# A transformer block, forward and backward, on one core: key weights on ScalarE's queue, transposes inside the key products, grad_out products in M's buffers, two norms on ScalarE

## The chip, the core and the metric

The kernel runs on one core of one Trainium2 chip. A core has five engines that run at the same time: TensorE (PE in the profile, with its weight loads as PEld), VectorE (DVE), ScalarE (ACT), GpSimd (POOL) and SyncE (SP). Each takes its own instructions in program order. TensorE writes to PSUM; the others read PSUM or SBUF. Transfers between HBM and SBUF are issued by SP, ACT or POOL, each on a queue of its own. The metric is the device time of one execution, in microseconds (us).

## The reference

One block without batch: S = 2048 rows, D = 640 columns, H = 32 heads of 20, F = 1728; bf16 throughout.

```python
h   = x + A(layernorm(x))
out = h + B(layernorm(h))
# A: linear attention
q, k, v = split(xn @ wqkv)               # per head
phi(t)  = where(t > 0, t + 1, exp(t)) + 1e-6
kv, z   = phi(k)^T v, sum of phi(k)      # over all rows, per head
A       = (phi(q) kv / (phi(q) z + 1e-6)) @ wo
# B: gated MLP
B       = (silu(hn @ w1) * (hn @ w3)) @ w2
```

The outputs are `out` and the gradients of x, wqkv, wo, w1, w3 and w2 for a given grad_out.

## The kernel before

The rows are cut into ST = 16 tiles of P = 128, the 640 columns into DT = 5 blocks of 128 or two halves of HD = 320. The order of all instructions is written out by hand (`manual_schedule`): what stands first in the program is first on its engine. The parts that the change touches are three.

**Phase 1, from 0 to about 55 us** (the loop over t at line 480). x is loaded tile by tile. For each tile DVE computes mean and variance (`Stats.part`: two `bn_stats`, one `bn_aggr`, the epsilon), POOL the inverse root (`pow`, line 154), and DVE normalises the tile in place (`p1_norm`, line 160); the even tiles above 8 are normalised by ACT instead (`norm_act`, line 165), which needs a bias from POOL (`Stats.bias`). The normalised tile is transposed: tiles 0 to 7 by PE and a copy on ACT (`p1_tr`), tiles 8 to 15 by a transposing DMA on SP's queue (in `p1_norm`). Then come the key product (`p1_mm`, tile name big, line 260) and `phi`: exp and relu on ACT, and two steps on DVE that are held back and done in a later turn (`held`, `phi_rest`). M = pk^T xn is accumulated over all tiles (`m_part`, macc, line 402). PE also does four query tiles (`q_tile`) in this loop, and four chunks of the product grad_out w2^T (`ghh_chunk`, tile gp, line 371), whose operands g2T and w2T come by transposing DMAs.
The PSUM buffers here are the tags big (2, each of two banks), tr (2) and m (2). The gp chunks take a big buffer, and the WARM matmuls on a tile of ones, ahead of everything, take a tr buffer. SP's queue at the start is: x tiles 0 and 1, the two halves of the key weights (`load_wq(2, 3)`, `load_wq(3, 4)`, line 182), x tiles 2, 3 and 4 to 7, w2T, g2T, w2T, further x and weights.

**The end of the attention, from about 90 to 103 us** (`run(...)` at line 801). `f2_half(t, j)` computes one half of tile t of h on PE. For tiles 0 to 3, half 0 is added to x by DVE; for half 1 PE adds x through an identity matmul and ACT copies the result (line 589). DVE takes the statistics; `f2_hn(t)` normalises (DVE, line 160), `f2_ht(t)` transposes on PE (trh, line 677), and ACT copies that (line 678).

**The backward pass through the MLP, from about 406 to 543 us** (the loop over t at line 1112). `b_ghn(t)` accumulates 27 blocks from ggb, which holds the gradients of two tiles and has two buffers, in parts of 9 matmuls. The next ggb comes in two loads on SP's queue: blocks 0 to 13 (FT = 14) at even t, blocks 14 to 26 at odd t. ACT has in each step the evacuation gs, y (line 1024, `ln_rest`), the transposing DMA of g_h (`b_gT`) and, in the first ten of them, one of wo or kvT.

## Time and profile before

| | |
|---|---|
| median of 4 runs | 826.88 us (826.28 to 836.13) |
| the profiled execution | 828.8 us |
| its span | 827.1 us |
| TensorE busy | 818.4 us, 99% |
| DVE, ACT, POOL busy | 454.2, 319.0, 133.8 us |
| TensorE's waits over 0.05 us that the profile names | 4.8 us in all |
| DMA moved | 157.59 MB, mean 191 GB/s |

The span runs from the first to the last instruction on the chip. Busy time is the union of an engine's instructions; matmul ends are modelled, and a matmul that runs at a lower clock counts as busy for longer. In a timeline each row gives start, length, engine, line, operation, how many were merged, and in brackets how long the engine had been idle and what ended that. Engine names with a q are the engine's sequencer, which issues transfers. A wait for several things is put down to the one that came last.

### The profile page before, as it was taken

The numbers are of one execution on the slowest core, as the hardware profiler recorded it, in microseconds if no ns is written. First come the engines' busy times: TensorE is split into PE (matmuls) and PEld (weight loads), VectorE is DVE, ScalarE is ACT, GpSimd is POOL, SyncE is SP. The second block draws the span as 40 slices with busy tenths as digits, with TensorE's granted clock in tenths as the row PEclk, the third lists the DMA queues.
The fourth block names the chain that finished last, engine by engine and source line by source line (L and its number), as shares of the span: only waits on it lengthen the run. The fifth ranks groups of instructions, "written<-read, shape, count | busy, mean of one in ns | idle before, by whom it ended". The sixth has DMA issues, their size and how long they took to land.

```text
span 827.1 us, 14217 instructions
## 1 busy us (share of the span) xinstructions
PE 818.4 (99%) x5551; PEld 523.7 (63%) x5551; DVE 454.2 (55%) x960; ACT 319.0 (39%) x609; POOL 133.8 (16%) x196
## 2 busy tenths in 40 slices
PE   8999999999999999999999999999999999999998
PEld 5677644555555555777777777777777777555554
DVE  7849898899898656400057777772681545200000
ACT  5865778655555666011121221222212333211111
POOL 2326333233222212100001111110220000000000
PEclk9999999999999999999999999999999999999999
DMA  9789999696584465999978888458995788885781
GB/s 250 216 289 211 259 244 278 221 213 168 143 204 133 144 202 166 204 253 235 258 163 186 184 217 199 72 103 178 264 216 100 163 191 172 215 194 139 159 174 38
DMA packets 318339, 157.59 MB, mean 191 GB/s; under 512 B 235456, under 2 KB 311456, under 8 KB 318272
## 3 DMA queue, kind: packets, MB, share of 16 engines
q1 hardware_dynamic: 286256, 120.65, 63.6%
q0 software_dynamic: 7376, 24.81, 8.8%
q10 hardware_dynamic: 24640, 11.23, 6.6%
q8 instruction: 43, 0.70, 0.4%
q14 instruction: 24, 0.20, 0.1%
HBM read 48.15 MB, written 51.46 MB: 120 GB/s over the span
## 4 chain that ended last, share of the span: by engine, by line
PE 96%; DMA 2%; SPq 1%; ACT 0%; DVE 0%; issue 0%; POOL 0%; ACTq 0%
PE mm L371 20%; PE job L1198 19%; PE ghn L1000 14%; PE gxn L1356 8%; PE o L766 7%; PE gw L955 7%; PE big L260 4%; PE gwo L1085 3%; PE gr L1057 3%; PE dkv L1302 3%; PE macc L402 3%; PE at L586 2%; PE mm L260 1%; DMA g2T<-in_grad_out_dram 1%; DMA pqT<-pql 1%; PE gp L371 1%
## 5 line engine op out<-in xcount | busy, mean ns | idle before, releaser
L1198 PE MATMUL job<-gb,hnN 128*128 128x432 bf16 (+2 forms) x656 | 117.0, 342 | 0.0
L1000 PEld LDWEIGHTS <-ggb 128*128 128x128 bf16 x864 | 84.5, 98 | 32.8
L1198 PEld LDWEIGHTS <-hnN 128*128 128x128 bf16 x656 | 63.6, 98 | 53.4
L371 PE MATMUL mm<-pqT,w 128*128 128x512 bf16 x405 | 93.7, 379 | 0.0
L371 PEld LDWEIGHTS <-w 128*128 128x128 bf16 x540 | 52.5, 98 | 63.0 <-issue 1.0
L1202 ACT CAST obs<-job 128x432 bf16<-128x432 f32 (+3 forms) x61 | 29.3, 480 | 123.1 <-PE job L1198 123.1
L766 PE MATMUL o<-w,hhT 128*128 128x320 bf16 x448 | 67.5, 299 | 0.0
L1000 PE MATMUL ghn<-w13a,ggb 128*128 128x320 bf16 x448 | 63.5, 299 | 0.0
L1000 PE MATMUL ghn<-w13b,ggb 128*128 128x320 bf16 x416 | 61.4, 299 | 0.0
L371 PE MATMUL mm<-g2T,w2T 128*128 128x512 bf16 x240 | 59.6, 379 | 0.0
L766 PEld LDWEIGHTS <-hhT 128*128 128x128 bf16 x448 | 43.8, 98 | 23.6
L955 PE MATMUL gw<-g,hb 128*128 128x320 bf16 x416 | 56.8, 299 | 0.0
L1065 POOL TENSOR_TENSOR sz<-Zb,g_h 128x640 f32<-128x640 bf16 x16 | 20.2, 1261 | 199.3 <-DVE g_h L1063 199.3
L955 PEld LDWEIGHTS <-hb 128*128 128x128 bf16 x416 | 40.6, 98 | 16.0 <-issue 0.3
L1356 PE MATMUL gxn<-wqT,gT 128*128 128x320 bf16 x320 | 48.7, 299 | 0.0
L391 ACT CAST ghh<-mm 128x512 bf16<-128x512 f32 x48 | 28.1, 585 | 46.2 <-PE mm L371 40.6
L705 ACT ACTIVATE sig<-mm 128x512 bf16<-128x512 f32 x56 | 33.5, 599 | 27.9 <-PE mm L371 25.6
L371 PEld LDWEIGHTS <-w2T 128*128 128x128 bf16 x260 | 25.4, 98 | 26.1 <-issue 3.2
L1012 ACT ACTIVATE gs<-ghn 128x640 bf16<-128x640 f32 x16 | 11.2, 703 | 79.0 <-PE ghn L1000 79.0
L260 PE MATMUL big<-wqkv,pqT 128*128 128x320 bf16 x260 | 39.7, 301 | 1.0 <-ACT pqT L256 0.6
L260 PEld LDWEIGHTS <-pqT 128*128 128x128 bf16 x320 | 30.7, 98 | 14.3 <-ACT pqT L256 2.1
L1356 PEld LDWEIGHTS <-gT 128*128 128x128 bf16 x320 | 31.3, 98 | 12.2
(201 smaller groups left out, 1284.6 us busy)
## 6 DMA issues: line engine op xcount, KB each, us to landing
hh_d<-hhT SPq DMA_DIRECT2D x24, 256.0 KB, 2.6
gg_d<-gate POOLq DMA_DIRECT2D x24, 256.0 KB, 4.0
gg_d<-ghh POOLq DMA_DIRECT2D x24, 256.0 KB, 3.4
ggb<-gg_d SPq DMA_DIRECT2D x6, 896.0 KB, 5.4
ggb<-gg_d SPq DMA_DIRECT2D x6, 832.0 KB, 7.3
x_sb<-in_A_x_dram SPq DMA_DIRECT2D x7, 640.0 KB, 6.9
out_dram<-obs ACTq DMA_DIRECT2D x39, 108.0 KB, 3.1
ggb<-gg_d SPq DMA_DIRECT2D x2, 1728.0 KB, 13.2
```

Of the source, the lines that this page charges most:

```text
L260: T.matmul(acc, lhsT=pqT[:, c, t * P:(t + 1) * P], rhs=wqkv[:, c, n0:n0 + HD], start=(c == 0), stop=(c == DT - 1))
L371: T.matmul(acc[:], lhsT=w[:, c, fc * P:(fc + 1) * P], rhs=rhs[:, c, :], start=(c == 0), stop=(c == DT - 1))
L391: A.copy(out=ghh[n // 2][:, n % 2, :], in_=acc[:])
L402: T.matmul(macc[m][j][:, 0:n], lhsT=pk_all[:, t, m * P:(m + 1) * P], rhs=x_ext[:, t, j * HD:j * HD + n], start=(t == 0), stop=(t == ST - 1))
L705: A.activation(sig[:, i, :], gp[:], AF.Sigmoid)
L766: T.matmul(o2["ps"][:, 0:HD], lhsT=hhT[c][:, fc, i * P:(i + 1) * P], rhs=w2[:, fc, j * HD:(j + 1) * HD], start=(fc == 0), stop=(fc == FT - 1))
L955: T.matmul(acc[:, j, 0:HD], lhsT=hb[b][:, t, i * P:(i + 1) * P], rhs=g2[:, t, j * HD:(j + 1) * HD], start=(t == 0), stop=(t == ST - 1))
L1000: T.matmul(acc[:, j, 0:HD], lhsT=ggb[t // 2][:, k, lo:lo + P], rhs=rhs[:, j * HD:(j + 1) * HD], start=(k == 0), stop=(k == NG - 1))
L1057: T.matmul(gr[t][:, j, 0:HD], lhsT=ghT[t][:, c, :], rhs=wT2[:, c, j * HD:(j + 1) * HD], start=(c == 0), stop=(c == DT - 1))
L1198: T.matmul(acc[:, 0:n], lhsT=lhs[:, t, m * P:(m + 1) * P], rhs=rhs(t), start=(t == 0), stop=(t == ST - 1))
L1202: A.copy(out=ob, in_=acc[:, 0:n])
L1356: T.matmul(acc[:, j, 0:HD], lhsT=g, rhs=wqT[:, k, j * HD:(j + 1) * HD], start=(k == 0), stop=(k == 14))
```

## The change

- The key weights are loaded in two halves from ACT's queue (`load_wk`), ahead of ACT's table load, and no longer from SP's. On SP's queue x tiles 8 to 11 come before the second w2T load.
- WARM falls from 44 matmuls to 34, followed by 8 more after the transposes of tile 0; they take an m buffer.
- Tile 0 is only centred before its transposes (256 columns by DVE, 384 by ACT with a bias `nmean`); exp and relu apply the scale for it (`RAW = 1`), and DVE scales the tile in place at t = 3 (`p1_scale`).
- The transposes of tile t + 1 stand between the two halves of key product t, for all of tiles 1 to 7.
- The order of DVE's steps in the loop (statistics S, norm N, phi's steps R, the scale C, norms on ACT A) is a table, `v_steps`. The four gp chunks come at t = 3 to 6 and not at 2 to 5, and take an m buffer; the first query tile comes at t = 6; M's products begin at t = 7 with three tiles, then three, then one per turn. The first w1 and w3 loads come one turn later.
- `Stats.bias` is one POOL instruction and not two.
- Half (2, 0) of `f2_half` is done ahead of (0, 1); `f2_hn(1)` and `f2_hn(2)` are done by ACT.
- In the backward loop the load of blocks 14 to 26 of ggb is issued from ACT's queue, in the middle of odd turns, after `ln_rest` and `b_gT`.

```diff
@@ -162,12 +162,12 @@
 
         def norm_act(self, out, src, t):
 
-            A.activation(out=out, in_=src, func=AF.Identity, bias=self.nb[t][:, 1:2], scale=self.rs[:, t:t + 1])
+            A.activation(out=out, in_=src, func=AF.Identity, bias=self.nb[t][:, 0:1], scale=self.rs[:, t:t + 1])
 
         def bias(self, t):
-            nb = self.nb[t] = cp.tile([P, 2], F32, name="nb", bufs=4)
-            G.tensor_tensor(out=nb[:, 0:1], in0=self.mv[:, t, 0:1], in1=self.rs[:, t:t + 1], op=ALU.mult)
-            G.tensor_tensor(out=nb[:, 1:2], in0=zero[:], in1=nb[:, 0:1], op=ALU.subtract)
+            nb = self.nb[t] = cp.tile([P, 1], F32, name="nb", bufs=4)
+            G.tensor_scalar(out=nb[:], in0=self.mv[:, t, 0:1], scalar1=self.rs[:, t:t + 1], scalar2=-1.0, op0=ALU.mult,
+                            op1=ALU.mult)
 
     ln1, ln2 = Stats("ln1"), Stats("ln2")
 
@@ -184,10 +184,13 @@
     def load_x(a, b):
         dma(out=x_sb[:, a:b, :], in_=xS[:, a:b, :])
 
+    def load_wk(j):
+        A.dma_start(out=wqkv[:, :, D + j * HD:D + (j + 1) * HD], in_=wq_v[:, :, D + j * HD:D + (j + 1) * HD])
+
+    load_wk(0)
     load_x(1, 2)
+    load_wk(1)
     A.activation(sg[:], zero[:], AF.Exp)
-    load_wq(2, 3)
-    load_wq(3, 4)
     load_x(2, 3)
     load_x(3, 4)
     load_x(4, 8)
@@ -235,7 +238,8 @@
     Z = cp.tile([P, DT], F32, name="Z")
 
     XT_DMA = 8
-    WARM = 44
+    WARM = 34
+    RAW = 1
 
     def on_act(t):
         return t > XT_DMA and t % 2 == 0
@@ -255,15 +259,21 @@
 
             A.copy(out=pqT[:, a:b, t * P:(t + 1) * P], in_=tr[:, a:b, :])
 
+    def p1_scale(t):
+        xn = x_sb[:, t, :]
+        V.tensor_scalar(out=xn, in0=xn, scalar1=ln1.rs[:, t:t + 1], scalar2=None, op0=ALU.mult)
+
     def p1_half(acc, t, n0):
         for c in range(DT):
             T.matmul(acc, lhsT=pqT[:, c, t * P:(t + 1) * P], rhs=wqkv[:, c, n0:n0 + HD], start=(c == 0),
                      stop=(c == DT - 1))
 
-    def p1_mm(t, n0):
+    def p1_mm(t, n0, between=None):
         acc = ps.tile([P, 2, 512], F32, name="big", bufs=2)
         for j in range(2):
             p1_half(acc[:, j, 0:HD], t, n0 + j * HD)
+            if j == 0 and between is not None:
+                between()
         return acc
 
     def two(ap):
@@ -271,17 +281,16 @@
 
     held = []
 
-    def phi(acc, dst, then=None):
+    def phi(acc, dst, t):
 
         mq, rq = (p1.tile([P, D], BF16, name=n, bufs=b) for n, b in (("mq", 3), ("rq", 3)))
-        A.activation(two(mq[:]), acc[:, :, 0:HD], AF.Exp)
-        A.activation(two(rq[:]), acc[:, :, 0:HD], AF.Relu)
+        kw = dict(scale=ln1.rs[:, t:t + 1]) if t < RAW else {}
+        A.activation(two(mq[:]), acc[:, :, 0:HD], AF.Exp, **kw)
+        A.activation(two(rq[:]), acc[:, :, 0:HD], AF.Relu, **kw)
 
         def rest():
             V.tensor_scalar(out=mq[:], in0=mq[:], scalar1=1.0, scalar2=1e-6, op0=ALU.min, op1=ALU.add)
             V.tensor_tensor(out=dst, in0=mq[:], in1=rq[:], op=ALU.add)
-            if then is not None:
-                then()
         held.append(rest)
 
     def phi_rest(keep=0):
@@ -303,7 +312,7 @@
 
     def q_tile(t):
         q_home(t)
-        phi(p1_mm(t, 0), pqs[t])
+        phi(p1_mm(t, 0), pqs[t], t)
 
     dz = {}
 
@@ -432,39 +441,59 @@
     zero_pads()
     load_w2T(0, 2 * P)
     load_g2T(0)
+    load_x(8, 12)
     load_w2T(2 * P, 4 * P)
-    load_x(8, 12)
     load_wq(0, 2)
     load_x(12, ST)
-    warm = ps.tile([P, 512], F32, name="warm", tag="tr", bufs=2)
-    for _ in range(WARM):
-        T.matmul(warm[:, 0:P], lhsT=ones[:], rhs=ones[:], start=True, stop=True, skip_group_check=True)
-    ln1.run(x_sb, 0, 1)
-    ln1.part(x_sb, 1, 0)
-    for a, b in ((0, 2 * P), (2 * P, D)):
-        ln1.norm(x_sb[:, 0, a:b], x_sb[:, 0, a:b], 0)
+    def warm_up(n):
+        warm = ps.tile([P, 512], F32, name="warm", tag="m", bufs=2)
+        for _ in range(n):
+            T.matmul(warm[:, 0:P], lhsT=ones[:], rhs=ones[:], start=True, stop=True, skip_group_check=True)
+
+    warm_up(WARM)
+    def center(t, a=0, b=D):
+        ln1.center(x_sb[:, t, a:b], x_sb[:, t, a:b], t)
+
+    nmean = cp.tile([P, 1], F32, name="nmean")
+
+    def center_first():
+        V.tensor_scalar(out=nmean[:], in0=ln1.mv[:, 0, 0:1], scalar1=-1.0, scalar2=None, op0=ALU.mult)
+        center(0, 0, 2 * P)
+        A.activation(out=x_sb[:, 0, 2 * P:], in_=x_sb[:, 0, 2 * P:], func=AF.Identity, bias=nmean[:, 0:1])
+
+    def stat(t):
+        ln1.run(x_sb, t, t + 1)
+        if on_act(t):
+            ln1.bias(t)
+
+    ln1.part(x_sb, 0, 0)
+    ln1.part(x_sb, 0, 1, center_first)
     p1_tr(0, ((0, 2), (2, DT)))
-    for t in (1, 2):
-        if t == 1:
-            ln1.part(x_sb, t, 1)
-            p1_norm(t)
-            ln1.run(x_sb, t + 1, t + 2)
-        else:
-            ln1.part(x_sb, t + 1, 0)
-            p1_norm(t)
+    warm_up(8)
+    stat(1)
+    ln1.part(x_sb, 2, 0)
+    p1_norm(1)
+    ln1.part(x_sb, 2, 1)
+    ln1.part(x_sb, 3, 0)
+    p1_norm(2)
     ln1.part(x_sb, 3, 1)
+    ln1.part(x_sb, 4, 0)
+    p1_norm(3)
+    ln1.part(x_sb, 4, 1)
     w13 = [go for c0, c1 in ((0, 2), (2, 4), (4, 5)) for go in load_w13(c0, c1)]
     w13 += [lambda: dma(out=w1[:, :, F:FP], in_=rows(B_w3)[:, :, F - FL:F])]
 
     def load_wo():
         dma(out=wo[:], in_=A_wo.rearrange("(c p) n -> p c n", p=P))
 
-    trickle = {3: w13[0], 4: w13[1], 11: lambda: load_wq(4, 6), 12: w13[2], 14: w13[3], 15: load_wo}
-
-    stat_of = {t: (t + 4,) for t in range(7)}
-    stat_of.update({7: (11, 12), 8: (13,), 9: (14,), 10: (15,)})
-    norm_of = {t: (t + 3,) for t in range(8)}
-    norm_of.update({8: (11, 12), 9: (13,), 10: (14,), 11: (15,)})
+    trickle = {4: w13[0], 5: w13[1], 11: lambda: load_wq(4, 6), 12: w13[2], 14: w13[3], 15: load_wo}
+
+    R = None
+    v_steps = {1: (R, ("N", 4)), 2: (("S", 5), R, ("N", 5)), 3: (("S", 6), R, ("N", 6), ("C", 0)),
+               4: (("S", 7), R, ("N", 7), ("S", 8)), 5: (R, ("N", 8), ("S", 9)), 6: (R, ("N", 9), ("S", 10)),
+               7: (("S", 11), R, R, ("A", 10), ("N", 11)), 8: (("S", 12), R, R, ("S", 13), ("A", 12)),
+               9: (("N", 13), R, ("S", 14)), 10: (R, R, ("S", 15), ("A", 14)), 11: (("N", 15), R)}
+    V_OPS = {"S": stat, "N": p1_norm, "C": p1_scale}
 
     def xn_out(g, q):
         sl = slice(g * TPC, (g + 1) * TPC)
@@ -476,30 +505,26 @@
 
     outs = {6: ((group_out, 0),), 7: ((xn_out, 0, dma),), 10: ((group_out, 1), (xn_out, 1, dma)), 13: ((group_out, 2),)}
 
-    QT = (5, 7, 9, 11)
+    QT = (6, 7, 9, 11)
+    M0 = {7: (0, 1, 2), 8: (3, 4, 5)}
+    M0.update({t: (t - 3,) for t in range(9, ST)})
     for t in range(ST):
-        k = p1_mm(t, D)
-        if t < 3:
-            p1_tr(t + 1, ((0, 2), (2, DT)))
-        for n in stat_of.get(t, ()):
-            ln1.run(x_sb, n, n + 1)
-            if on_act(n):
-                ln1.bias(n)
-        for n in norm_of.get(t, ()):
-            if not on_act(n):
-                p1_norm(n)
-        phi_rest(t < 4)
-        phi(k, pk_all[:, t, :])
-        for n in norm_of.get(t, ()):
-            if on_act(n):
-                p1_norm(n)
+        k = p1_mm(t, D, (lambda: p1_tr(t + 1)) if t + 1 < XT_DMA else None)
+        steps = v_steps.get(t, (R,) * len(held))
+        for step in steps:
+            if step is R:
+                held.pop(0)()
+            elif step[0] != "A":
+                V_OPS[step[0]](step[1])
+        phi(k, pk_all[:, t, :], t)
+        for step in steps:
+            if step is not R and step[0] == "A":
+                p1_norm(step[1])
         if t in QT:
             q_tile(QT.index(t))
-        if 2 <= t < 6:
-            ghh_chunk(t - 2, ps.tile([P, 2, 512], F32, name="gp", tag="big", bufs=2)[:, 0])
-            p1_tr(t + 2)
-        if t >= 3:
-            m_part(0, [t - 3])
+        if 3 <= t < 7:
+            ghh_chunk(t - 3, ps.tile([P, 512], F32, name="gp", tag="m", bufs=2))
+        m_part(0, M0.get(t, ()))
         if t >= 11:
             V.memset(bd[:, t - 11, :], 0.0)
             make_mask(t - 11)
@@ -658,10 +683,14 @@
         pqs[t] = pf.tile([P, D], BF16, name="pql", bufs=4)[:]
         dma(out=pqs[t], in_=pq_v[:, t, :])
 
-    def f2_hn(t):
+    def f2_hn(t, on_act=False):
         hn[t] = (pf.tile([P, D], BF16, name="hn", tag="pql", bufs=4) if 2 <= t < TPC else
                  pf.tile([P, D], BF16, name="hn", bufs=2))
-        ln2.norm(hn[t][:], x_sb[:, t, :], t)
+        if on_act:
+            ln2.bias(t)
+            ln2.norm_act(hn[t][:], x_sb[:, t, :], t)
+        else:
+            ln2.norm(hn[t][:], x_sb[:, t, :], t)
         dma(out=hn_v[:, t, :], in_=hn[t][:])
 
     def f2_ht(t):
@@ -802,8 +831,8 @@
         (q_late, 12, lambda: (f2_wT(0), f2_wT(1))), (q_late, 13, lambda: (f2_wT(2), f2_wT(3))), (phi_rest,),
         (q_late, 14, lambda: f2_wT(4)), (load_x, 4, 8), (r_head, 5), (r_prod, 7), (r_store, 5, 6), (f2_m_out,),
         (f2_w_out,), (q_out, 8, 10), (q_out, 10, 14), (load_w2T, 8 * P, 10 * P), (mlp_ghh, 4), (q_late, 15),
-        (sig_table,), (f2_half, 0, 0), (f2_half, 1, 0), (f2_half, 0, 1), (f2_half, 1, 1), (f2_hn, 0), (mlp_ghh, 5),
-        (f2_half, 2, 0), (f2_hn, 1), (load_w2T, 10 * P, F), (f2_half, 2, 1), (f2_ht, 0), (f2_half, 3, 0), (f2_hn, 2),
+        (sig_table,), (f2_half, 0, 0), (f2_half, 1, 0), (f2_half, 2, 0), (f2_half, 0, 1), (f2_half, 1, 1), (f2_hn, 0),
+        (mlp_ghh, 5), (f2_hn, 1, True), (load_w2T, 10 * P, F), (f2_half, 2, 1), (f2_ht, 0), (f2_half, 3, 0), (f2_hn, 2, True),
         (f2_half, 3, 1), (f2_ht, 1), (mlp_ghh, 6), (f2_hn, 3), (f2_ht, 2), (r_red, 6), (r_inv, 6), (r_scale, 6), (r_T, 6),
         (f2_half, 4, 0), (f2_ht, 3), (mlp_ghh, 7), (f2_half, 4, 1), (r_red, 7), (r_inv, 7), (r_scale, 7), (r_T, 7),
         (r_store, 6, 8))
@@ -927,10 +956,10 @@
 
     ggb = {}
 
-    def load_gg(j, c0, c1):
+    def load_gg(j, c0, c1, q=dma):
         if c0 == 0:
             ggb[j] = ba.tile([P, NG, 2 * P], BF16, name="ggb", bufs=2)
-        dma(out=ggb[j][:, c0:c1, :],
+        q(out=ggb[j][:, c0:c1, :],
             in_=gg_d[c0 * P:c1 * P, j * 2 * P:(j + 1) * 2 * P].rearrange("(c p) w -> p c w", p=P))
 
     def gw2_tail():
@@ -1116,8 +1145,8 @@
             next(g, None)
 
         u = t - 2
-        if 2 <= t <= ST - 3:
-            load_gg(t // 2 + 1, *((FT, NG) if t % 2 else (0, FT)))
+        if 2 <= t <= ST - 3 and t % 2 == 0:
+            load_gg(t // 2 + 1, 0, FT)
         part()
         part()
         part()
@@ -1127,6 +1156,8 @@
             ln_rest.pop(t - 1)()
             if by_dma(t - 1):
                 b_gT(t - 1)
+            if 2 <= t <= ST - 3 and t % 2:
+                load_gg(t // 2 + 1, FT, NG, A.dma_start)
             if t <= 2 * DT:
                 n = (t - 1) % DT
                 dst, src = (woT, A_wo) if t <= DT else (kvN, kvT_d)
```

## The prediction

> **What bounds the kernel now.** I read the busy shares first, then TensorE's (PE's) waits, then the first 20 us slice by slice.
>
> ```profile
> PE 818.4 (99%) x5551; PEld 523.7 (63%) x5551; DVE 454.2 (55%) x960; ACT 319.0 (39%) x609; POOL 133.8 (16%) x196
> ```
>
> PE is busy in all but 8.7 of 827.1 us, and the change takes away only two of its 5551 matmuls. So it can win only idle time, or time in which PE runs slowly and still counts as busy. PE's waits:
>
> ```profile
> PE gp L371 <- DMA g2T<-in_grad_out_dram: 2.0, 1, 2.0
> PE warm L441 <- DVE zero L124: 1.1, 1, 1.1
> PE trh L677 <- DVE hn L160: 0.7, 1, 0.7
> PE big L260 <- ACT pqT L256: 0.6, 2, 0.3
> PE at L586 <- DMA Wp<-pkx: 0.4, 1, 0.4
> ```
>
> The first is the largest: the first grad_out product (gp, line 371) waits for its transposed operand. The windows of 1 us (PE, PEld, DVE, ACT, POOL busy; granted clock; DMA share; GB/s) show its second cost:
>
> ```profile
> 13.00:14.00 1.00, 0.27 (x5) 0.10 (x2) 0.93 (x5) 0.86 (x3) 0.17 (x1) 1.00 1.19 160
> 14.00:15.00 1.00, 0.00 (x0) 0.00 (x0) 1.00 (x3) 1.00 (x2) 0.68 (x1) 1.00 0.99 35
> 15.00:16.00 1.00, 0.76 (x2) 0.29 (x3) 0.93 (x5) 0.10 (x1) 0.35 (x1) 0.55 1.16 265
> 16.00:17.00 1.00, 1.00 (x4) 0.40 (x3) 0.89 (x3) 0.00 (x0) 0.33 (x1) 0.50 0.82 259
> ```
>
> Column 8 is the clock: it fell to half after the hole and is full again in the slice from 19. Five gp matmuls took 2.29 us there, 1.24 later; with the transposes and matmuls beside them that is 1.7 us more. VectorE (DVE) is busy in nearly every slice here, so it is what comes next. From 20 to 90 us PE has no hole above 0.11 us.
>
> **Part 1: loads at the start.** Now SyncE (SP) issues everything in order:
>
> ```profile
> 4.29 3.16 SPq L430 DMA_TRANSPOSE w2T<-in_B_w_dram  x1
> 7.51 4.24 SPq L223 DMA_TRANSPOSE g2T<-in_grad_out_dram  x1
> 11.79 1.40 SPq L430 DMA_TRANSPOSE w2T<-in_B_w_dram  x1
> ```
>
> g2T lands 7.6 us after its issue begins, at 15.11. Moving the two key-weight loads (L182, 0.99 us with their gap 1.04) to ScalarE's (ACT's) queue brings g2T's issue to 6.45 and its landing to 14.1. On ACT the two issues (0.4 to 0.5 us each) come ahead of the table load, which then ends at 3.1 instead of 2.1; ACT is first wanted at 4.5, so that costs nothing.
> Against this stands a rule of the Trainium skill (DMA: Bandwidth & Descriptors, "Issuing engines are not separate DMA queues"): loads issued from several engines run on the same 16 DMA engines and interleave, so only issue time is saved. The trace agrees where it can: from 4 to 9 us the DMA share is 1.05 or more at 318 to 358 GB/s, with one queue alone. By the row of issues I win the 1.04 us; by the rule no more than that, and the first x tile now shares its time with 400 KB of weights. Before, it landed at 3.13 with nothing beside it. Its delay lies between 0 and 1.3 us (400 KB at 318 GB/s); I take 0.25, since its 160 KB are few packets of a mix, and keep 1.3 for the range.
>
> **Part 2: the first tile.** It is now only centred (no wait for POOL's pow, 0.57 us), 256 columns on DVE and 384 on ACT, and phi applies the scale. The second half of its transposes moves from 5.85 to about 5.5, the first key product from 6.37 to about 6.2. WARM 34 + 8: 34 at 0.107 us end at 4.75, where the clock rose in the trace; no price.
>
> **Part 3: the loop.** In the new order PE does the transposes of tile t+1 inside key product t, the grad_out products come at t = 3 to 6, M's first products at t = 7, and the M buffers take the grad_out accumulators. What paces it is DVE: per tile two statistics 0.92, aggregate 0.24, epsilon 0.07, norm 0.36, and from t = 1 phi's two steps 0.83 (starts to starts). From the first statistics at 3.4 I get the norms of tiles 1, 2, 3, 4 at about 7.25, 9.2, 11.2 and 13.25, and of 5, 6, 7 at 15.6, 18.0, 20.8. In the trace they are:
>
> ```profile
> 12.32 0.44 DVE L160 TENSOR_SCALAR x_sb<-x_sb,ln_mv,ln_rs 128x640 bf16<-128x640 bf16 x1
> 13.90 0.44 DVE L160 TENSOR_SCALAR x_sb<-x_sb,ln_mv,ln_rs 128x640 bf16<-128x640 bf16 x1
> 15.49 0.44 DVE L160 TENSOR_SCALAR x_sb<-x_sb,ln_mv,ln_rs 128x640 bf16<-128x640 bf16 x1
> ```
>
> (tiles 3, 4, 5). So DVE's chain is hardly faster; the win is order. PE: tile 4's transposes at 13.75, key product 3 done at 14.75, the first gp right then with g2T there since 14.1, done at 15.85. In the trace the same work (key products 0 to 3, transposes 0 to 4, one gp) is done at 19.6 + 0.3. **Win: 4.0 us**, and the ACT hole of 0.11 at 35 us too: 4.1. Afterwards PE is the pace again (key product 1.36, transposes 0.28, gp 1.08 against DVE's 2.4 per tile).
> Does it last? Tile 8's transposed x is wanted at 28.7, issued at 23.6 and lands in 2.6 to 3.8 us; tile 9's has about 1 us left, tile 15's 3. The next far cover is mT for kvT_block(0): it landed at 67.0 and was used at 68.9. SP's chain there starts from ACT's norm of tile 14 (42.4), which comes 3.8 us earlier, so 1.6 us of cover remain. No new stall; if one, under 1 us. The two nb instructions on POOL become one (0.2 to 0.4 us, hidden).
>
> **Part 4: norms 1 and 2 of the second layernorm on ACT.** The reordered half (2,0) covers the Wp wait: -0.4. But ACT is first in, first out, and each norm now stands ahead of the copy of the next tile's half, on which the next statistics wait. On the trace's clock: epsilon of tile 1 ends at 95.65, pow 0.55, the new bias 0.2 to 0.4 on POOL, so ACT's norm starts at 96.6. Its length:
>
> ```profile
> 33.08 0.92 ACT L165 ACTIVATE x_sb<-x_sb,nb,ln_rs 128x640 bf16<-128x640 bf16 x1
> ```
>
> It holds the copy of half (2,1), ready at 96.0, until 97.4 and DVE's statistics until 97.85; so pow at 98.9, norm 2 on ACT 99.8 to 100.7, the copy of (3,1) behind it 100.6 to 101.0, statistics, pow, and hn(3) at 103.1. PE wants hn(2) at 99.2 and waits 1.5, then hn(3) and waits 1.5 again. In the trace the last transposes (trh) start at 101.33, now at 103.15: **loss 1.8 us**, the 0.4 counted in. That these norms save DVE 0.7 us wins nothing, as DVE then waits for ACT.
> Does the clock fall in these two holes? The Trainium skill (TensorE: Matmul & The Clock Gate, "What's actually happening") says that it drops after a whole idle window of about 3.4 us, and then the holes cost nothing more. The trace disagrees: one hole of 1.98 us sufficed, and cost 1.7. Two holes of 1.5 with 1.0 us of work between are near that row. Ends 0 and 1.7; I take 0.8, as it hangs on where the window falls. **Loss in all: 2.6.**
>
> **Part 5: second halves of ggb on ACT's queue.** Each of the six is 832 KB:
>
> ```profile
> ggb<-gg_d SPq DMA_DIRECT2D x6, 896.0 KB, 5.4
> ggb<-gg_d SPq DMA_DIRECT2D x6, 832.0 KB, 7.3
> ```
>
> SP issues them far ahead (424.9, landed 432.4, used at 442.2). On ACT they stand behind y and the ghT transpose of their step, and ahead of woT's:
>
> ```profile
> 434.72 1.22 ACTq L1037 DMA_TRANSPOSE ghT<-g_h  x1
> 435.98 1.30 ACTq L1133 DMA_TRANSPOSE woT<-in_A_wo_dram  x1
> 442.22 1.25 PE L1000 MATMUL ghn<-w13b,ggb 128*128 128x320 bf16 x8
> ```
>
> So issue at 435.98 and use at 442.2: 6.2 us, 9.8 us of cover becoming about 1. By the first halves' row (5.4 us, little beside them) it lands at 441.2 to 441.4, at no cost; by its own row (7.3 us, measured with the other half and the ghT transpose in flight) 1.1 us late. I take the first, since at 436 to 438.6 SP's queue is empty. The woT issue behind it delays nothing that PE waits for within a step; ghT of the odd steps lands sooner, also hidden.
>
> **Sum.** -4.1 + 1.8 + 0.8 = -1.5 us. The profiled execution took 828.8 (span 827.1 and 1.7 around it), so 827.3 there; the median of the runs, 826.88, stands 1.9 below it, and I forecast **825.4 us**.
>
> **Rivals.**
> - *ACT's norms are hidden after all* (chance 0.22): bias and copies slip between, and PE's waits of 0.7 and 0.4 go. -4.1 - 1.1: 821.7. For it: ACT is idle 0.4 to 0.9 us before most copies there. Against: strict order on ACT.
> - *The start wins little* (0.13): x shares the DMA engines with the weights and lands 1.3 us later, DVE with it, or the clock is not warm. -2.0 + 2.6: 827.5. For it: the DMA share at 1.
> - *ggb lands late* (0.15), the other side: at its own row's 7.3 us PE stalls 1.1 us in each of six pairs, a stall in one pair not helping the next: +6.6 - 1.5 = +5.1: 832.0. It decides from 6.2 us to landing on; at 7.9 us it is +8.7.
> - *The change doesn't do what it says* (0.02): the M buffers' reuse makes key products wait; about 827.
> - The forecast (0.48): 823.5 to 827.5.
>
> **Range and chances.** The range reaches from the first rival with the start's best (about 820.5) to the ggb rival's middle (830.5). A measurement of this kernel can tell about 1%, 8.3 us, from no change. Faster by that needs nearly all of PE's 8.7 idle us back: 0.04. Slower by that needs ggb at about 8 us and the rest as forecast: 0.08. Within: 0.88.
>
> **What would show it.** Right: no g2T wait on PE, full clock in the slices from 15 to 19, gp first near 14.8; ACT's two norms near 92 and 95 on the new clock with PE's trh waits at about 3 us; no wait for ggb. Wrong: PE waiting for the key weights or pqT before 10 us; PE waits on ggb (then slower); trh waits under 1 us (then near 822); a wait for mT near 64.

## The result and the profile after

The changed kernel takes **831.11 us** (median of 44 runs, 828.88 to 837.97) against 826.99 us before (63 runs): slower by 0.5%, ratio 1.0049 with a 95% interval of 1.0038 to 1.0061. The forecast was 825.4 us with a range to 830.5: it is wrong in sign, and the result lies 0.6 us outside the range.

The profiled execution took 835.1 us (span 833.4, mean granted clock 0.996) and lies above its median, so it shows more trouble than most runs have. What divides the runs is TensorE's granted clock: 28 of the 44 runs keep a mean of 0.999 or more and have a median of 830.14 us, the other 16 lie at 832.66. Of the 67 runs of the kernel before that were timed beside the first four experiments, 61 keep 0.999 or more (826.73 us). All sums below use this split. In the 18 profiles it is exact: the seven with a mean under 0.999 hold a stretch at half clock, the eleven others none between 8 us and the last 10.

First line of the busy shares after:

```profile
PE 820.3 (98%) x5549; PEld 524.0 (63%) x5549; DVE 452.8 (54%) x959; ACT 322.0 (39%) x609; POOL 133.6 (16%) x195
```

TensorE has two matmuls fewer, as counted, but is idle or slow for longer. Its waits after (line, cause: us in total, times, longest):

```profile
PE trh L706 <- DVE hn L160: 3.5, 1, 3.5
PE trh L706 <- ACT hn L165: 1.6, 1, 1.6
PE warm L451 <- DVE zero L124: 1.1, 1, 1.1
PE ghn L1029 <- DMA ggb<-gg_d: 0.9, 1, 0.9
PE tr L258 <- DVE x_sb L160: 0.6, 1, 0.6
PE big L268 <- DMA pqT<-x_sb: 0.5, 1, 0.5
PE mm L268 <- ACT mbs L418: 0.4, 1, 0.4
```

The wait for g2T is gone. In its place stand 5.1 us of trh waits in the stage with the two norms on ACT, a wait for ggb, one of the transposes of tile 1 (tr) for its norm at 7.6 us, and waits for pqT and mbs; the kernel before had no such waits but 0.7 us of trh. The start went as forecast. Windows after (PE, PEld, DVE, ACT, POOL busy; clock; DMA share; GB/s), and SP's rows (start, length of the issue):

```profile
14.00:15.00 1.00, 1.00 (x13) 0.77 (x11) 0.97 (x4) 1.00 (x3) 0.00 (x0) 1.00 1.09 345
15.00:16.00 1.00, 1.00 (x7) 0.49 (x6) 0.86 (x5) 1.00 (x3) 0.56 (x1) 1.00 1.15 98
16.00:17.00 1.00, 1.00 (x10) 0.69 (x9) 1.00 (x4) 1.00 (x2) 0.00 (x0) 1.00 2.56 182
```

```profile
3.37 3.59 SPq L439 DMA_TRANSPOSE w2T<-in_B_w_dram  x1
7.01 3.75 SPq L226 DMA_TRANSPOSE g2T<-in_grad_out_dram  x1
```

TensorE is full where it had a hole, at full clock. g2T landed at 12.83 (forecast 14.1), the first gp started at 15.08 (14.75), the norms of tiles 1 to 4 at 7.68, 9.61, 11.55 and 13.58 (7.25, 9.2, 11.2, 13.25). At the key product of tile 9, where both orders have done the same of TensorE's work but for two warm-up matmuls, the changed kernel was 3.8 us ahead of the profile of before (31.39 us against 35.23).

The end of the attention is where it was lost. First ACT before, where the copy out of PSUM (the CAST, line 589) follows PE at once (brackets: idle before, and what ended it), then ACT after, then DVE after:

```profile
96.58 0.42 ACT L589 CAST x_sb<-at 128x320 bf16<-128x320 f32 x1 [0.91 <-PE at L586]
98.35 0.42 ACT L589 CAST x_sb<-at 128x320 bf16<-128x320 f32 x1 [0.75 <-PE at L586]
```

```profile
95.01 0.92 ACT L165 ACTIVATE hn<-x_sb,nb,ln_rs 128x640 bf16<-128x640 bf16 x1 [1.02 <-POOL nb L169]
95.84 0.40 ACT L614 CAST x_sb<-at 128x320 bf16<-128x320 f32 x1
98.23 0.92 ACT L165 ACTIVATE hn<-x_sb,nb,ln_rs 128x640 bf16<-128x640 bf16 x1 [1.39 <-POOL nb L169]
99.06 0.40 ACT L614 CAST x_sb<-at 128x320 bf16<-128x320 f32 x1
```

```profile
96.28 0.49 DVE L147 BATCH_NORM_STATS2 st<-x_sb 128x6 f32<-128x320 bf16 x1 [2.07 <-ACT x_sb L614]
99.49 0.49 DVE L147 BATCH_NORM_STATS2 st<-x_sb 128x6 f32<-128x320 bf16 x1 [1.37 <-ACT x_sb L614]
103.30 0.45 DVE L160 TENSOR_SCALAR hn<-x_sb,ln_mv,ln_rs 128x640 bf16<-128x640 bf16 x1 [2.88 <-DMA pqT<-pql]
```

Each norm waits at the head of ACT's queue for POOL's bias nb, and the copy (now line 614), whose input is long ready, stands behind it; DVE's next statistics wait for that copy. The third DVE row is something the forecast did not have: hn(3) lies in a buffer of tag pql, and the transposing DMA of r(5) was still reading it. That DMA needed 13.0 us here:

```profile
L370 SPq DMA_TRANSPOSE pqT<-pql x1: 1300/1300/1300, 90.1 to 90.1; - x1
DMA to landing us min/median/max: 13.0/13.0/13.0
```

And behind the long hole the clock (third number from the right) is at half until 109.4:

```profile
101.00:102.00 1.00, 0.00 (x0) 0.00 (x0) 0.00 (x0) 0.14 (x1) 0.05 (x1) 1.00 1.03 250
102.00:103.00 1.00, 0.00 (x0) 0.00 (x0) 0.00 (x0) 0.00 (x0) 0.00 (x0) 0.76 1.26 215
104.00:105.00 1.00, 1.00 (x7) 0.61 (x6) 0.93 (x4) 0.45 (x1) 0.00 (x0) 0.50 1.13 337
```

Against the profile of before a lead of 2.4 us at 92 us became a lag of 2.5 at the last trh and, with the slow clock, of 5.2 when the clock was full again in the MLP.

### The profile page after: what moved, and what is told of

It reads as the page before. It is cut to its first block, busy times and chain, and to the rows that moved or that the text cites. A ratio compares the mean times of both kernels' runs of the same rounds, so it can differ in the third digit from the quotient of the medians.

```text
span 833.4 us, 14221 instructions
## 1 busy us (share of the span) xinstructions
PE 820.3 (98%) x5549; PEld 524.0 (63%) x5549; DVE 452.8 (54%) x959; ACT 322.0 (39%) x609; POOL 133.6 (16%) x195
## 4 chain that ended last, share of the span: by engine, by line
PE 90%; DMA 4%; DVE 3%; ACT 1%; issue 0%; POOL 0%; SPq 0%; ACTq 0%; DVEq 0%
PE mm L380 20%; PE job L1229 19%; PE ghn L1029 13%; PE gxn L1387 8%; PE o L795 7%; PE gw L984 7%; PE gwo L1114 3%; PE dkv L1333 3%; PE gr L1086 2%; PE at L611 2%; PE big L268 2%; PE macc L411 2%; DMA pqT<-pql 2%; DMA ggb<-gg_d 1%; DVE st L147 1%; DMA x_sb<-in_A_x_dram 1%
```

## The experiments

Each is timed against the kernel before on the same chip; "at full clock" means the runs with a granted clock of 0.999 or more. Between the chips the kernel before differs by up to 0.25 us at full clock (826.70 to 826.95), so differences of that size between experiments on different chips are not read. Line numbers shift by a few where a kernel differs.

### The parts alone

**The start alone** (e1_start). The changed loop and loads; the order of halves, the norms and the ggb loads as before. Against the changed kernel:

```diff
-        (f2_half, 1, 0), (f2_half, 2, 0), (f2_half, 0, 1), ... (f2_hn, 1, True), ... (f2_hn, 2, True),
+        (f2_half, 1, 0), (f2_half, 0, 1), ... (f2_half, 2, 0), (f2_hn, 1), ... (f2_hn, 2),
-        if 2 <= t <= ST - 3 and t % 2 == 0:
-            load_gg(t // 2 + 1, 0, FT)
+        if 2 <= t <= ST - 3:
+            load_gg(t // 2 + 1, *((FT, NG) if t % 2 else (0, FT)))
-            if 2 <= t <= ST - 3 and t % 2:
-                load_gg(t // 2 + 1, FT, NG, A.dma_start)
```

> The change's start and loop alone: the end of the attention in the old order with norms on DVE, ggb on SP's queue. Theory 1 (the start wins, the ACT norms lose): the trace of the changed kernel is 2.4 us ahead of before when it reaches the first halves of h at 91 us, so about 824.6 us, with no half clock at 104. Theory 2 (the faster start itself pulls the transfers together, so that hn(3) waits for its buffer whatever engine does the norms): 827 to 830 us, with DVE waiting over 1 us at hn(3) for the transposing DMA of tile 5.

**The order and the norms on ACT alone** (e2_f2). The first two lines of that diff the other way round, on the kernel before, with the one-instruction bias.

> Before, with only the new order of halves and the norms of tiles 1 and 2 on ACT. Theory 1: trh waits of 1.5 us or more for hn(2) and hn(3), so 2 us more without and 3.5 to 4.5 with a fall of the clock: 829 to 831 us. Theory 2: the chain over ACT costs at most 1.5 us, no wait for a DMA at hn(3): 827 to 828.5 us.

**ggb alone** (e3_gg). The last lines of that diff the other way round, on the kernel before.

> Before, with only the second halves of ggb issued from ACT's queue. By the trace of the changed kernel, where five of six loads landed in time and the last, with three xn loads beside it, 0.9 us late: 0 to 0.9 us more, 827 to 828 us. By the prediction's rival (1.1 us in each of six): 833.5 us.

**The change with both norms on DVE** (e4_dve_norms).

```diff
-        (mlp_ghh, 5), (f2_hn, 1, True), ... (f2_hn, 2, True),
+        (mlp_ghh, 5), (f2_hn, 1), ... (f2_hn, 2),
```

> The changed kernel with the norms of tiles 1 and 2 back on DVE, the new order of halves kept. Theory 1: the two trh waits shrink to 0.7 us or less in all and the clock stays full: 824 to 825.5 us. Theory 2: the norms' engine is not what costs; hn(3) still waits for its buffer: 828 us or more.

| kernel | median us | ratio to before (95%) | at full clock |
|---|---|---|---|
| start alone | 827.00 | 1.0003 (0.9990 to 1.0016) | 826.91 |
| order and ACT norms alone | 829.67 | 1.0032 (1.0021 to 1.0044) | 828.77 |
| ggb alone | 827.55 | 1.0004 (0.9988 to 1.0020) | 827.52 |
| change, norms on DVE | 827.58 | 1.0001 (0.9987 to 1.0014) | 827.59 |

Taking the norms off ACT gives back 3.5 of the 4.1 us. The start, on which the forecast put a gain of 4.1, wins nothing, so the numbers that rested on it (824.6, and 824 to 825.5) were missed. (827.00 lies where theory 2 of the start alone put it, but the wait of hn(3) for its buffer, which that theory named, is not in the profile.) Both e2_f2 and e3_gg keep the start of before, and their profiles say why. TensorE's wait at the first gp and two windows, in e2_f2:

```profile
PE gp L371 <- DMA g2T<-in_grad_out_dram: 0.9, 1, 0.9
```

```profile
15.00:16.00 1.00, 1.00 (x11) 0.75 (x10) 0.93 (x5) 0.61 (x3) 0.40 (x1) 1.00 0.82 248
16.00:17.00 1.00, 1.00 (x9) 0.71 (x8) 0.89 (x3) 0.61 (x2) 0.27 (x1) 1.00 1.06 365
```

With the same instructions as before the hole is 0.9 us and not 2.0, and the clock stays at 1.00. So it is in e3_gg and in a later kernel with that start (e11_before_late), both at full clock:

```profile
PE gp L371 <- ACT mq L277: 1.3, 1, 1.3
PE gp L371 <- DMA g2T<-in_grad_out_dram: 1.1, 1, 1.1
```

In these three g2T took 6.6 to 6.9 us from issue to landing, in the profile of before 7.6; in e3_gg the gp matmul then waited a little longer for its PSUM buffer, which ACT was still reading. Matched instruction by instruction, e2_f2 and e3_gg are 2.7 and 2.4 us ahead of the profile of before at 20 us, with the start unchanged. So the profiled execution of before was one of the rare runs with a half-clock stretch, and 2.3 to 2.7 us of the 4.0 that the start was to win lay in it. What is left is a lead of 1.2 to 1.6 us at the key product of tile 9, and it is given back. TensorE's waits from 23 to 78 us in the start alone:

```profile
PE big L268 <- DMA pqT<-x_sb: 0.8, 2, 0.5
PE mm L268 <- ACT mbs L418: 0.4, 1, 0.4
```

Against e3_gg the start alone is 1.6 us ahead at the key product of tile 9 at 31 us, 1.0 at 35 (after a wait of 0.49 for the transposed tile 10), 0.3 at 48 (after 0.26 for tile 15) and 0.25 behind at 76 (after 0.38 for mbs). Counted from start to start of the matmuls, these three waits and one of 0.07 for tile 12 took 0.66, 0.43, 0.54 and 0.23 us, which is all of it. The same four points against e11_before_late in a last kernel (e16_nb_early) read 1.2 and 0.7 ahead, 0.0, and 0.55 behind.

### Does the lead get lost whatever its size?

**The start alone, delayed** (e8_delay).

```diff
+            for _ in range(24 if t == 3 else 0):
+                T.matmul(gp[:, 0:P], lhsT=ones[:], rhs=ones[:], start=True, stop=True, ...)
             ghh_chunk(t - 3, gp)
```

> The start alone (x loop and loads as changed, the later stages as before), with 24 matmuls of 128 columns of ones put ahead of the first grad_out product at 15 us: they delay TensorE by about 1.3 us there and do nothing else. Their results are overwritten. Theory 1 (the start is really about 1.3 us earlier in most executions, but the lead is given back to the waits for the transposing DMA of tiles 10 and 15 and for mbs): the three waits shrink by what is added, and the median stays at 827.0 (within 0.5). Theory 2 (the lead at 28 us reaches the end, and the start wins nothing because it was nothing): 828.3, 1.3 us above the start alone.

Measured 832.78 us (ratio 1.0075, 1.0049 to 1.0101; 830.93 at full clock, from two runs): neither theory. The delay was 1.3 us, as built, and at tile 10 its wait took 0.66 of it back. But then everything behind it met something else (waits in e8_delay):

```profile
PE trh L709 <- DVE hn L160: 2.3, 1, 2.3
PE at L614 <- DMA Wp<-pkx: 2.0, 1, 2.0
PE big L268 <- DMA pqT<-x_sb: 1.3, 1, 1.3
```

The last transpose of Wp was issued at 88.71 and took 4.4 us (2.6 us in the start alone, at 87.17), r(5) was issued 1.2 us behind the first of POOL's four stores there and took 10.7 us. So TensorE's time at 88 us is no slack: arriving later there costs several times the delay.

**The same delay with POOL's stores moved** (e12_delay_late): as above, with these four stores (`f2_m_out`, `f2_w_out`, both `q_out`) behind `f2_hn(3)`.

> The start alone, with the 24 matmuls of ones ahead of the first grad_out product (1.3 us later at 15 us; they cost 5.8 us at the end) and with POOL's four stores moved behind hn(3). Theory 1 (the delay cost so much because it moved SP's transposing DMAs of Wp and r(5) into POOL's stores, at 88 to 103 us): the waits for Wp (2.0 us) and at hn(3) (2.3 us) and the half clock go, and the median is 827 to 828.5. Theory 2 (the delay is paid elsewhere): above 831.

Measured 830.07 us (1.0036, 1.0021 to 1.0050), between the two. The wait at hn(3) fell to 0.6, so that part was POOL's stores; the wait for Wp stayed at 2.1 us, so that part was not, and its cause stays open. In this profile the clock is at half behind that wait, from 94.2 to 97.6 us.

### The buffer of hn(3), and POOL's stores

**An own buffer** (e5_own_hn).

```diff
-        hn[t] = (pf.tile([P, D], BF16, name="hn", tag="pql", bufs=4) if 2 <= t < TPC else
+        hn[t] = (p1.tile([P, D], BF16, name="hn3", tag="rq", bufs=3) if t == 3 else
+                 pf.tile([P, D], BF16, name="hn", tag="pql", bufs=4) if t == 2 else
```

> The changed kernel, with one edit: hn(3) lies in a buffer that has been free since q_late 13 (the ring of rq) and no longer in one of tag pql, which the transposing DMA of r(5) still reads. Both ACT norms stay. Theory 1 (two costs: the two waits for ACT's norms, 1.6 us each of which the second is covered by the first's delay, and on top of them the wait of hn(3) for that DMA with the half clock that follows): the 3.5 us wait of trh on hn(3) falls to under 1 us, no slice at half clock, and the median falls from 831.1 to about 829.2. Theory 2 (hn(3) is late because the chain before it is late; its buffer is no cost of its own in a typical execution): median within 0.7 us of 831.1. Theory 3 (the buffer is the whole cost, ACT's norms cost nothing): about 827.5, the time with both norms on DVE.

**POOL's stores late** (e9_stores_late). The changed kernel with this move, which e12_delay_late has too:

```diff
-        (r_store, 5, 6), (f2_m_out,), (f2_w_out,), (q_out, 8, 10), (q_out, 10, 14), (load_w2T, 8 * P, 10 * P),
+        (r_store, 5, 6), (load_w2T, 8 * P, 10 * P),
-        (f2_hn, 3), (f2_ht, 2),
+        (f2_hn, 3), (f2_m_out,), (f2_w_out,), (q_out, 8, 10), (q_out, 10, 14), (f2_ht, 2),
```

> The changed kernel with one move: POOL's four large stores (f2_m_out, f2_w_out and both q_out, which it issues from 89.7 to 92.7 us, 3 us of its own time, and which carry 200 to 380 GB/s until 103) come after f2_hn(3) in the order, at about 99 us. Both ACT norms stay. Theory 1 (the transposing DMA of r(5) is starved by these stores, hn(3) waits for its buffer, and ln_rs and nb on POOL stand behind the issue of the stores): r(5) lands within 5 us of its issue, the wait at hn(3) is under 1 us, no slice at half clock, and the median falls from 831.1 to 829 or below; what stays is the two waits behind ACT's norms. Theory 2 (the cost is ACT's queue alone): 830.2 to 831, the median of the executions that keep the full clock.

Both removed the long wait and neither helped: 832.13 us (1.0069, 1.0044 to 1.0095) and 831.72 us (1.0052, 1.0040 to 1.0064). The waits in e5_own_hn, the same to 0.1 us in e9_stores_late:

```profile
PE trh L707 <- ACT hn L165: 1.6, 1, 1.6
PE trh L707 <- DVE hn L160: 1.3, 1, 1.3
```

These two are what the norms on ACT cost in an ordinary run. The wait of 3.5 us for the buffer belongs to the profiled run and others like it, and is not what moves the median: without it 3 of 6 and 10 of 21 runs still fell under a clock of 0.999. Of the expectations theory 2 is nearest in both, but the times lie above it. Both kernels are even 1 us slower than the changed one at full clock (831.10 from 3 runs, 831.21 from 11); in e9_stores_late 0.7 us of that is in longer waits for ggb, the rest is open.

The stores moved in **the start alone** (e10_start_late) and in **the kernel before** (e11_before_late):

> The start alone (norms of the later stage on DVE in the old order) with the same move of POOL's four stores. Theory 1: hn(0) no longer waits for ln_rs behind the stores' issue (0.6 us at 92.7), and the 0.8 us wait of trh goes: 826.2, 0.8 below the start alone, the best of the versions so far. Theory 2 (the stores come to stand in the way of the loads of the next stage instead): 827 or above.

> The kernel before with the same move of POOL's four stores and nothing else. Theory 1: 826.0, the 0.7 us wait of trh gone. Theory 2 (the stores collide with what follows): 827 or above.

827.31 us (1.0003, 0.9987 to 1.0018) and 827.02 us (0.9998, 0.9981 to 1.0015): no gain in either.

### One norm at a time

**Only hn(1) on ACT** (e6_act1: `(f2_hn, 2, True)` becomes `(f2_hn, 2)`) and **only hn(2) on ACT** (e7_act2: `(f2_hn, 1, True)` becomes `(f2_hn, 1)`).

> The changed kernel with hn(2) back on DVE; only hn(1) is normalised on ACT. Theory 1 (each norm on ACT adds its own wait of 1.5 us, and the DMA wait comes when hn(3) meets POOL's stores): about 829.0, with one trh<-ACT hn or copy wait of some 1.6 us and at most 1 us at hn(3). Theory 2 (it is the pair that costs, one ACT norm is hidden): 827.6, the time with both on DVE. Theory 3 (it is this first norm, beside the stores of POOL, that makes it all): 831.

> The changed kernel with hn(1) back on DVE; only hn(2) is normalised on ACT. Theory 1 (each norm adds its own wait): about 829.0, the wait of trh on hn(2) 1.5 us. Theory 2 (only the pair costs): 827.6. Theory 3 (the first norm makes it all): 827.6 here with 831 when the first is alone.

830.13 us (1.0036, 1.0023 to 1.0049) and 828.90 us (1.0029, 1.0018 to 1.0040), against 827.58 with none and 831.11 with both: each has its price, 2.5 and 1.3 us, and the sum is near that of the pair. (At full clock it is 2.1, from three runs, and 1.25, against 2.55 for the pair.) e6_act1 shows how little idle time the clock needs. Its two trh waits were 0.96 and 0.81 us, 1.0 us of work between:

```profile
97.00:98.00 1.00, 0.04 (x2) 0.04 (x2) 0.96 (x4) 0.68 (x2) 0.27 (x1) 1.00 1.09 423
98.00:99.00 1.00, 1.00 (x10) 0.65 (x10) 0.68 (x3) 0.54 (x1) 0.18 (x1) 1.00 1.01 392
99.00:100.00 1.00, 0.19 (x3) 0.09 (x3) 0.59 (x2) 0.15 (x1) 0.37 (x1) 1.00 1.01 398
100.00:101.00 1.00, 1.00 (x7) 0.64 (x8) 0.93 (x4) 0.43 (x1) 0.00 (x0) 0.53 1.23 304
```

The clock is at half from 100 to 103.5, and matched to the version with both norms on DVE that costs about 1.6 us. e5_own_hn had waits of 1.6 and 1.3 us in the same place and kept full clock.

The 18 traces hold the time of every change of the clock, and they show why. Within a trace all changes lie whole multiples of 3.413 us apart, on a grid that starts at another point in each execution. The seven half-clock stretches in mid-kernel last 3.413 us (five of them, as 15.09 to 18.51 before and 100.05 to 103.46 here) or twice that (two, as 102.53 to 109.35 after). What counts is all of TensorE's idle time inside one window of this grid (between the matmuls' modelled ends and the next starts):

| profile | window, us | idle in it, us | clock after it |
|---|---|---|---|
| e14_start_order | 612.81 to 616.22 | 2.22 | half |
| e12_delay_late | 90.81 to 94.22 | 2.06 | half |
| e15_norm_behind | 97.22 to 100.63 | 1.97 | full |
| e8_delay | 91.31 to 94.72 | 1.86 | full |
| before | 11.68 to 15.09 | 1.85 | half |
| e6_act1 | 96.64 to 100.05 | 1.77 | half |
| e13_gg_sp | 95.41 to 98.82 | 1.69 | full |
| e5_own_hn | 95.53 to 98.95 | 1.64 | full |

Of all windows at full clock up to 815 us, the five with more than 2.0 us idle were followed by half clock, those with less than 1.7 never; between 1.77 and 1.97 it went either way. The two holes of e6_act1 lay in one window, those of e5_own_hn in two. From this comes an estimate: with the holes of e13_gg_sp (97.06 to 98.70 and 99.82 to 101.08 us), the grid brings 1.77 us into one window in 48% of its positions and 1.97 us in 37%. The five kernels with both ACT norms ahead of the copies fell under 0.999 in 44 of 99 runs, from 1 of 6 (e13_gg_sp) to 14 of 22 (e2_f2), the changed kernel in 16 of 44. That agrees in the main; where the runs without a profile lost their clock is not shown, and the kernel before loses it in 6 of 67.

### ggb, and the new order

**ggb back on SP in the changed kernel** (e13_gg_sp) and **the start with the new order of halves, norms on DVE, ggb on SP** (e14_start_order). Both have the ggb lines of the first diff, e14_start_order also `(f2_hn, 1)` and `(f2_hn, 2)`.

> The changed kernel with the second halves of the six ggb loads back on SP's queue; everything else as changed. Theory 1 (the halves on ACT's queue cost 0.7 us, as they did alone on the kernel before, in waits of ghn for ggb): no wait for ggb, and the median falls from 831.1 to 830.4. Theory 2 (they cost nothing, and the 0.7 was noise): 831.1 (within 0.4).

> The start and the new order of halves, with both norms on DVE and all ggb loads on SP. Theory 1 (the order costs nothing, ggb on ACT 0.7): 826.9, as the start alone. Theory 2 (the order costs the 0.6 us that part the version with DVE norms from the start alone, and ggb nothing): 827.6.

829.47 us (1.0030, 1.0019 to 1.0041; 829.39 at full clock) and 827.30 us (1.0019, 1.0003 to 1.0034; 826.94 at full clock). The profile of e14_start_order (830.68 us) has its half clock at 616 us, behind a wait of 2.7 us in a stage that the change leaves alone. ggb on ACT's queue costs 0.65 to 0.8 us at full clock by three pairs: 827.52 - 826.73, 827.59 - 826.94 and 830.14 - 829.39. The intervals alone would not carry so small a difference; the traces do. All eight profiles with ggb on ACT show waits of ghn for ggb, 0.3 to 1.6 us in sum; those with ggb on SP show none. In the profile of the changed kernel it is one load of six:

```profile
ggb<-gg_d SPq DMA_DIRECT2D x6, 896.0 KB, 6.9
ggb<-gg_d ACTq DMA_DIRECT2D x6, 832.0 KB, 5.7
```

The median from issue to landing is 5.7 us and in time; the last load took 7.3 us, with three other loads beside it, and TensorE waited 0.9. The new order costs nothing at full clock (826.94 against 826.91).

### Which part of the ACT norm costs

**Each norm one step later** (e15_norm_behind), so that the copy of the next half is ahead of it:

```diff
-        (f2_hn, 1, True), (load_w2T, 10 * P, F), (f2_half, 2, 1), (f2_ht, 0),
-        (f2_half, 3, 0), (f2_hn, 2, True), (f2_half, 3, 1), (f2_ht, 1),
+        (load_w2T, 10 * P, F), (f2_half, 2, 1), (f2_hn, 1, True), (f2_ht, 0),
+        (f2_half, 3, 0), (f2_half, 3, 1), (f2_hn, 2, True), (f2_ht, 1),
```

> The changed kernel with each ACT norm issued one step later: hn(1) behind the second half of tile 2, hn(2) behind the second half of tile 3. ACT's queue then holds the copy out of PSUM (cast) that the next statistics need ahead of the norm and not behind it. Theory 1 (what costs is that this copy stands behind the norm, so DVE's statistics of the next tile wait 2.1 and 1.4 us): these two waits fall under 0.8 us, the waits of trh with them, and the median falls from 831.1 to about 828.5. Theory 2 (what costs is the norm's own path, statistics to POOL's nb to an ACT norm of 0.92 us where DVE's takes 0.45): 830.5 to 831.

830.54 us (1.0050, 1.0037 to 1.0063), theory 2 by the number. But the profile shows that it tested something else; ACT in e15_norm_behind:

```profile
93.91 0.42 ACT L614 CAST x_sb<-at 128x320 bf16<-128x320 f32 x1 [0.23 <-PE at L611]
96.21 0.92 ACT L165 ACTIVATE hn<-x_sb,nb,ln_rs 128x640 bf16<-128x640 bf16 x1 [1.87 <-POOL nb L169]
```

The copy is early now, at 93.91, but the bias had moved too: on POOL it stands behind the next tile's root, and the norm waits 1.87 us for it. TensorE then waits for the norms themselves:

```profile
PE trh L706 <- ACT hn L165: 3.5, 2, 2.2
```

**The same with the bias left in its place** (e16_nb_early): `ln2.bias` is called from the table and no longer in `f2_hn`; ggb on SP, so its neighbours are 829.47 (norms early) and 827.30 (norms on DVE).

```diff
-            ln2.bias(t)
+        (ln2.bias, 1), (load_w2T, 10 * P, F), (f2_half, 2, 1), (f2_hn, 1, True), (f2_ht, 0),
+        (f2_half, 3, 0), (ln2.bias, 2), (f2_half, 3, 1), (f2_hn, 2, True), (f2_ht, 1),
```

> The changed kernel with all ggb loads on SP (829.5 us by itself), with each ACT norm one step later as in the last experiment, but with POOL's bias nb left where it was, ahead of the next tile's statistics: in the last experiment nb had moved behind the next tile's ln_rs on POOL, and each norm waited 1.9 us for it. Theory 1 (what costs is the copy of the next half's sum out of PSUM, which stands behind the norm on ACT): DVE's waits of 2.1 and 1.4 us for that copy fall under 0.8, the waits of trh under 1 in sum, the median to about 827.8. Theory 2 (what costs is the norm's own path, from the statistics over two POOL operations to a norm of 0.92 us): 829.3 to 829.8, the waits of trh only moved from one tile to the next.

**826.70 us** (1.0014, 0.9998 to 1.0029; 826.68 at full clock; 3 of its 22 runs lie at 833 to 836). This is better than either theory had it. Both norms are on ACT with their full 0.92 us, and TensorE has no trh wait above 0.15 us left in the profile. ACT in e16_nb_early, and what DVE waits for from 92 to 106:

```profile
93.81 0.43 ACT L614 CAST x_sb<-at 128x320 bf16<-128x320 f32 x1 [0.23 <-PE at L611]
94.61 0.92 ACT L165 ACTIVATE hn<-x_sb,nb,ln_rs 128x640 bf16<-128x640 bf16 x1 [0.37 <-POOL nb L169]
96.01 0.42 ACT L614 CAST x_sb<-at 128x320 bf16<-128x320 f32 x1
96.33 0.92 ACT L165 ACTIVATE hn<-x_sb,nb,ln_rs 128x640 bf16<-128x640 bf16 x1
```

```profile
DVE st L147 <- ACT x_sb L614: 0.8, 2, 0.5
```

DVE's waits for the copy fell from 3.4 to 0.8 us. So the norms cost nothing by themselves. Their price was the order: a norm not yet ready stood ahead of a copy that was, or, in e15_norm_behind, its bias stood behind another root. No version of these beats the kernel before by more than the measurement can tell; this one equals it.

## Why the prediction was wrong, step by step

At full clock the parts are: start +0.2 (826.91 - 826.73), order 0.0 (826.94 - 826.91), norms on ACT +2.45 (829.39 - 826.94), ggb +0.75 (830.14 - 829.39), together +3.4. They form a chain of kernels from before to changed, so this sum closes by itself; what checks it are other kernels: ggb costs 0.8 and 0.65 in the two other pairs, and order and norms together cost 2.0 on the old start (828.77 - 826.73). The half clock in 16 of 44 runs lifts the median by another 1.0.

- **Part 3, the start: the step that failed.** Forecast -4.1, measured +0.2. The events came as drawn (gp at 15.08, full clock, no hole), so the mechanism was right and two terms were mis-sized. The 2.0 us hole with its half clock was taken as the kernel's, but three profiles with the same start have 0.9 to 1.3 us and no loss of clock. The text noted that the profiled execution stood 1.9 us above the median and then subtracted that from the end; it had to come off the stall. And "No new stall; if one, under 1 us" was wrong: pqT and mbs took the rest of the lead, 1.9 us from start to start in e1_start. It named the covers of tiles 8, 9 and 15; tiles 10 and 12, which ACT normalises, had none, and the 3 us given to tile 15 were not there either.
- **Part 4, the norms on ACT: right in mechanism and nearly in size.** Forecast 1.8 plus 0.8 for the clock; the 1.8 were 2.2 for the norms less 0.4 for the order of halves. Measured 2.45 for the norms at full clock, 0.0 for the order, and about 1.0 more in the median from the clock, which did hang on where the window falls. The two waits of TensorE were forecast at 1.5 each and are 1.6 and 1.3. The rival that had them hidden is out for this order, and true for another (e16_nb_early).
- **The buffer of hn(3): missing.** hn(2) and hn(3) reuse pql, and the transposing DMA that reads it landed with 1.9 us to spare in the trace of before (at 98.88, hn(3) at 100.83). It makes the profiled run slower but does not move the median.
- **Part 5, ggb: mis-sized by 0.75.** The forecast took 5.4 us to land and no cost; the median is 5.7, and one of six took 7.3, as the other end's row said. The rival that put 1.1 us on all six is out.
- **Part 1** came out early, but not as reckoned: g2T was issued at 7.01 and not 6.45, as the w2T issue ahead of it took longer (3.59 us, 3.16 before), so half of the queue's 1.04 us came; but it landed in 5.8 us and not 7.6, 1.3 us earlier than said. x tile 0 landed at 3.28 (0.15 late, 0.25 said).
- **Part 2** held at the first products (first key product at 6.48, 6.2 said), though the clock rose at 6.95 and not at 4.75; in the 18 profiles it rose between 3.9 and 7.2 us.

Errors of 4.3 for the start, 0.75 for ggb and 0.85 for norms and clock add up to 5.9; the miss was 5.7.

## What to carry to other kernels

Where a gain rests on one stall of one profiled execution, look first at how that execution stands to the median and at its granted clock: a run 1.9 us above the median at 0.998 may owe just that stall to itself. Whether a hole costs clock as well is chance: it is decided by the idle time that falls into one window of about 3.4 us, whose place the program does not set here, so give it a share of the runs and not a yes or no. On an engine that takes its work in order, put the operation that waits for a long chain behind the copies that others wait for, and leave its helper on the other engine where it was. A lead won early is worth only the smallest cover on the way to the end, so count every cover from the new time on.

## What the runs showed of the hardware

- The transposing DMA of r(5), 128x640 on SP's queue, took 6.5 to 7.9 us in 14 profiles, 10.7, 13.0 and 14.6 us in three, and 4.6 in e12_delay_late. In two of the three slow ones it was issued behind one or two of the stores; in the third (e2_f2, 14.6) ahead of them. With the stores moved away in the changed kernel it still took 6.9, behind a load on its own queue.
- The clock changed only on a grid of 3.413 us whose start differs between executions. It fell behind windows with 2.06 to 3.01 us idle (five of five), stayed full behind those with up to 1.69, and did either between 1.77 and 1.97 (two and two). It came back after one window, and after two where the first still held 1.27 or 1.49 us of idle time.
- A delay of 1.3 us at 15 us made the end 5.8 us later in the median (4.0 at full clock, from two runs).
